# Attention into a capacity-limited expert layer: the gate's VectorE steps moved within and across the slots of a hand-written order

## The chip, the cores and the metric

The kernel runs on one core of one Trainium2 chip. Each core has five engines with queues of their own, worked off in order: TensorE (PE; its weight loads are listed as PEld), VectorE (DVE), ScalarE (ACT), GpSimd (POOL) and SyncE (SP). SP and POOL issue most of the DMA transfers. The metric is the device time of one launch in microseconds; the median of three runs is given, and beside it one execution that was taken with the profiler.

## The reference

Inputs: q, k, v of shape (8, 12, 448, 64) (batch, heads, sequence, head size), gains g_q and g_k of 64, a gate matrix (768, 8), expert weights w1 (8, 768, 1024) and w2 (8, 1024, 768), capacity 80.

```
q_n = q / sqrt(mean(q*q) + 1e-6) * g_q          # the same for k
scores = q_n @ k_n.T / 8
attn = softmax(scores);  a = attn @ v            # (8, 12, 448, 64)
x = a, heads beside each other                   # (3584, 768)
logits = x @ w_gate;  expert = argmax(logits)
gate = max of softmax(logits)
per expert: of its tokens the 80 with the largest gate stay
    out[token] = gate * (relu(x[token] @ w1) @ w2)
all other rows of out are 0
```

## The kernel before, in words

**Groups, rows and slots.** The 96 heads are worked in 24 groups of four heads; three groups make a batch b, so there are 8 batches. A group has 7 rows (64 key positions for each of the two halves u). For a row, `score` (L351) computes transposed scores on PE into a PSUM tile ps, and ACT takes the exponential into an SBUF tile at (L362). `av` (L365) multiplies at with v on PE, added up over the 7 rows into po. `presum` (L387) adds up the at tiles on DVE into sm (L392, L394), whose column sums are the softmax denominators.

A **slot** s is two rows. The loop at L791 writes out, for each slot, in this order: the lists `begins`, the scores of rows 2s and 2s+1, the list `pre`, the presums of rows 2s-2 and 2s-1, the list `mid`, the av of those rows, then the lists `ahead` and `end`. Each engine's queue holds its instructions in the order in which they are written, so the place of a step in these lists is its place on every engine and DMA queue it uses. A list keeps the order in which steps were entered: first the loop over the groups (L717 to L734), then the loop over the batches (L735 to L764). So within one list of a slot a group's steps stand ahead of a gate's. There are 84 slots; group g starts in slot b0 = 7g//2.

**Preparing a group.** q and k are loaded on the SP queue (`load_qk`, L247). ACT squares them (`square`, L266, sq<-qk L270, list `mid` of slots b0-7 for q and b0-6 for k), DVE sums the squares (`squares`, L273, ms<-sq L278, list `end` of the same slots). `rstd` (L286, `mid` of slot b0-5) forms the inverse root: two ACT instructions (Ln L289, Exp L290, both called the root here) and three small DVE ones (L291 to L293). `normalise` (L300, qn, L306 on DVE) follows in the `mid` of b0-5 and b0-4. `transp` (L328, `end` of slot b0-2) turns qn on PE into tp, and ACT copies tp to qkT (L347, L349); for k the tp tile comes from the pool scps, which has two buffers and which the scores, the transposes of k and the merge's scratch tiles share.

**The gate of a batch.** With b0 = (3b+2)*7//2 (so 7, 17, 28, 38, 49, 59, 70, 80): `zl` (L396) forms gate sums and denominators on PE in slot b0+5, `gate1` (L414) copies them (zsb, zo) and adds them on DVE (zsb, L424), `gate1t` (L426, slot b0+6) turns them and ACT copies them to zs. `gate1v` (L439) forms the quotients on DVE: two reciprocals rz (L445) and four products lx (L453); it also issues two SP transfers of rz to DRAM (L460). `gate2` (L465) forms the logits: a reduction lg (L468), the maximum lmax (L471), lex (L474), eq (L476) and a small memset (L477). `gate2x` (L480) is the gate exponential on ACT (L481) and the copy of the kinds eqb (L483). `gate2b` (L486) sums and inverts it on DVE (lsum L489, gw L491). `gate2i` (L494) prepares tiles on POOL; `gate2p` (L515) splits gw on POOL (L518 to L512), waiting for gw.

**The merge.** `merge` (L524) keeps for each expert the 80 best tokens so far. Its steps: `row` (transposes of gw on PE, copied by ACT, L543), `experts` (`kinds`: transposes of eqb), `vbeat` (comparisons on DVE, L550, L553), `vtied` (ties, L559, L561), `own` and `vahead`, `counts` and `vput`, `place`, `turn`. The loop at L755 places them: the first function of a step in `ahead` (or `end` for `row`), the others in `end`.

**Weights.** The weights of experts 0 to 2 are loaded to SBUF by POOL (`fetch_held`, L669, behind a small DVE memset, L671). Those of experts 3 to 7 are first converted to bf16 in DRAM by POOL transfers of half a matrix (`stage_w`, L201, `begins`, 20 of them in slots 36 to 80: for matrix n, counted from 0, slots s = 9 + 23n//5 and s + 2), later fetched on SP.

**After the slots** comes the last batch's merge (L828 on), then the experts, one after the other.

The slot loop, and the functions that the diff touches:

Of the kernel before, what the change touches and what calls it, by code (L numbers as in the profile page):

```python
# [21 lines left out]
def kernel(  # L22
# [210 lines left out]
    with av_stack:  # L233
# [459 lines left out]
        begins, pre, mid, end = {}, {}, {}, {}  # L693

        def at_slot(where, s, f, *a):
            where.setdefault(s, []).append((f, a))
# [3 lines left out]
        def first(s, f, *a):  # L700
            ahead.setdefault(s, []).append((f, a))
# [15 lines left out]
        for g in range(NG):  # L717
            b0 = g * RD // 2
# [16 lines left out]
        for b in range(B):  # L735
            b0 = (NQ * b + NQ - 1) * RD // 2
            if b == B - 1:
                at_slot(end, b0 + 3, zl, b, range(NQ - 1))
                at_slot(end, b0 + 4, xout, NG - 2)
                at_slot(end, b0 + 4, zl, b, range(NQ - 1, NQ))  # L740
                at_slot(end, b0 + 4, gate1, b)
                at_slot(end, b0 + 4, xout, NG - 1)
                at_slot(end, b0 + 5, gate1t, b)
                at_slot(mid, b0 + 6, gate1v, b)
                continue
            first(b0 + 5, zl, b, range(NQ))
            first(b0 + 5, gate1, b)
            at_slot(end, b0 + 6, gate1t, b)
            at_slot(mid, b0 + 7, gate1v, b)
            at_slot(mid, b0 + 7, gate2, b)  # L750
            at_slot(mid, b0 + 8, gate2i, b)
            at_slot(end, b0 + 8, gate2x, b)
            at_slot(pre, b0 + 9, gate2b, b)
            at_slot(pre, b0 + 9, gate2p, b)
            for t, fs in enumerate(merge(b)):  # L755


                if b == B - 2 and t > 3:
                    at_slot(end, b0 + 12 + t, fs[0])
                    continue  # L760
                s = 15 + b % 2 if b < B - 2 else 13
                (first if t else lambda *a: at_slot(end, *a))(
                    b0 + (10, 10, 12, s, 18 + b % 2, 20 + b % 2)[t], fs[0])
                for n, f in enumerate(fs[1:]):  # L764
                    at_slot(end, b0 + (10, 11, 12, s)[t], f)
        at_slot(begins, 0, load_wgs)
        at_slot(end, NS - 6, weights_early)
        at_slot(end, NS, weights_late)
# [8 lines left out]
        for e in range(E):  # L777
            for i in range(2):
                s = 9 + 23 * (2 * e + i) // 5
# [48 lines left out]
    b = B - 1  # L828
# [215 lines left out]
```

## Time and profile before

| | |
|---|---|
| median of 3 runs | 423.92 us (422.47 to 424.89) |
| the profiled execution | 423.0 us |
| its span, first to last instruction | 421.3 us |
| PE busy | 399.1 us (95%) |
| DVE busy | 357.5 us (85%) |
| ACT busy | 314.9 us (75%) |
| POOL busy | 73.5 us (17%) |
| granted TensorE clock | 0.998 of full speed |
| HBM read and written | 335 GB/s over the span |

Busy time is the time with an instruction on an engine; register, semaphore and DMA-issuing instructions don't count. The slots of attention fill about the first 357 us, the last merge and the experts the rest. In the timelines that follow, a line is a run of like instructions: its start, the time to the end of its last, engine, line, operation, tiles, and in brackets the idle time before it with the engine and line that ended it. Instructions overlap a little at their ends, so a start may lie before the end of the one ahead. Times in the rows are microseconds from the start of the span.

### The profile page before, as it was taken

The numbers are of one execution on the slowest core, as the hardware profiler recorded it, in microseconds if no ns is written. First come the engines' busy times: TensorE is split into PE (matmuls) and PEld (weight loads), VectorE is DVE, ScalarE is ACT, GpSimd is POOL, SyncE is SP. The second block draws the span as 40 slices with busy tenths as digits, with TensorE's granted clock in tenths as the row PEclk, the third lists the DMA queues.
The fourth block names the chain that finished last, engine by engine and source line by source line (L and its number), as shares of the span: only waits on it lengthen the run. The fifth ranks groups of instructions, "written<-read, shape, count | busy, mean of one in ns | idle before, by whom it ended". The sixth has DMA issues, their size and how long they took to land.

```text
span 421.3 us, 12543 instructions
## 1 busy us (share of the span) xinstructions
PE 399.1 (95%) x5289; PEld 194.9 (46%) x5289; DVE 357.5 (85%) x641; ACT 314.9 (75%) x479; POOL 73.5 (17%) x118
## 2 busy tenths in 40 slices
PE   6799999999989999999899999999999999889993
PEld 6334444444444445444444444443444443448882
DVE  5699889998999999989999999989999779735550
ACT  5898979997889799979798799878997784202120
POOL 2000001301040205100420024001500050134321
PEclk9999999999999999999999999999999999999999
DMA  7355599999959999999799969999799298869981
GB/s 261 123 149 140 152 224 317 282 254 268 287 166 206 326 230 274 242 237 320 234 236 233 338 172 195 232 286 338 170 237 312 59 358 211 270 213 339 342 301 47
DMA packets 75983, 100.91 MB, mean 240 GB/s; under 512 B 8344, under 2 KB 65176, under 8 KB 75928
## 3 DMA queue, kind: packets, MB, share of 16 engines
q1 hardware_dynamic: 59856, 70.53, 52.2%
q0 software_dynamic: 15776, 29.13, 36.1%
q8 instruction: 41, 0.67, 0.6%
q10 hardware_dynamic: 296, 0.46, 0.4%
q14 instruction: 14, 0.11, 0.1%
HBM read 101.11 MB, written 39.89 MB: 335 GB/s over the span
## 4 chain that ended last, share of the span: by engine, by line
PE 69%; DMA 12%; DVE 10%; ACT 5%; issue 2%; SPq 0%; POOLq 0%; DVEq 0%; ACTq 0%
PE ps L359 26%; PE po L376 26%; DMA w_sb<-wb_scratch 5%; PE zl L411 4%; DMA qk<-in_k_dram 4%; PE tp L314 3%; PE xp L314 3%; DVE ms L278 2%; DVE sm L394 2%; DMA xr_scratch<-xb 2%; PE py L992 1%; DVE qn L306 1%; PE ph L973 1%; ACT qkT L349 1%; DMA xg<-xr_scratch,idxG 1%
## 5 line engine op out<-in xcount | busy, mean ns | idle before, releaser
L359 PE MATMUL ps<-qkT 64*64 64x448 f32 x1344 | 147.9, 548 | 7.6 <-ACT qkT L349 3.2
L362 ACT ACTIVATE at<-ps 128x896 f32<-128x896 f32 x168 | 146.4, 931 | 2.5 <-PE ps L359 1.6
L376 PE MATMUL po<-at,vt 64*64 64x448 f32 x1344 | 142.4, 537 | 0.1
L394 DVE TENSOR_TENSOR sm<-sm,at 128x896 f32<-128x896 f32 x120 | 132.0, 1100 | 2.9
L376 PEld LDWEIGHTS po<-at,vt 64*64 64x64 f32 x1344 | 50.0, 133 | 74.9 <-issue 64.3
L359 PEld LDWEIGHTS ps<-qkT 64*64 64x64 f32 x1344 | 43.1, 132 | 73.2 <-issue 23.5
L278 DVE TENSOR_REDUCE ms<-sq 128x14 f32<-128x896 f32 (+1 forms) x50 | 51.9, 1044 | 6.6 <-ACT sq L270 6.4
L306 DVE TENSOR_TENSOR qn<-qk,rs 128x896 f32<-128x896 f32 (+1 forms) x50 | 52.5, 1052 | 1.9
L270 ACT ACTIVATE sq<-qk 128x896 f32<-128x896 f32 (+1 forms) x50 | 46.3, 929 | 2.8 <-DMA qk<-in_q_dram 2.8
L518 POOL CAST pt<-gw 128x4 bf16<-128x4 f32 x8 | 6.9, 866 | 201.9 <-DVE gw L491 201.9
L977 ACT ACTIVATE h_sb<-ph 128x320 bf16<-128x320 f32 x16 | 7.0, 437 | 39.8 <-PE ph L973 39.8
L654 ACT COPY xb<-xp 128x1024 f32<-128x1024 f32 x24 | 24.3, 1011 | 9.7 <-PE xp L314 9.6
L314 PEld LDWEIGHTS tp<-ident,qn 64*128 64x128 f32 x672 | 23.4, 139 | 11.1 <-issue 5.3
L314 PE MATMUL tp<-ident,qn 64*128 64x64 f32 x672 | 26.9, 226 | 0.0
L383 ACT COPY us<-po 128x896 f32<-128x896 f32 (+1 forms) x24 | 21.4, 893 | 6.2 <-PE po L376 6.2
L392 DVE TENSOR_TENSOR sm<-at 128x896 f32<-128x896 f32 x24 | 25.9, 1081 | 0.0
L347 ACT ACTIVATE qkT<-tp,gqk 128x896 f32<-128x896 f32 x23 | 23.5, 1023 | 0.0
L349 ACT COPY qkT<-tp 128x896 f32<-128x896 f32 x24 | 21.9, 913 | 1.3 <-PE tp L314 1.2
L992 PE MATMUL py<-w_sb,h_sb 128*80 128x384 bf16 (+1 forms) x136 | 22.2, 317 | 0.6 <-DMA w_sb<-wb_scratch 0.6
L996 DVE TENSOR_SCALAR yo<-py,gwT 80x384 f32<-80x384 f32 (+1 forms) x16 | 9.5, 600 | 14.9 <-PE py L992 14.7
L411 PE MATMUL zl<-us,wgs 64*32 64x448 f32 x192 | 21.0, 540 | 0.0
L411 PE MATMUL zl<-sm,zsel 64*32 64x448 f32 x192 | 20.5, 540 | 0.0
(170 smaller groups left out, 412.0 us busy)
## 6 DMA issues: line engine op xcount, KB each, us to landing
wb_scratch<-in_moe_w_dram POOLq DMA_DIRECT2D x20, 768.0 KB, 14.9
w_sb<-wb_scratch SPq DMA_DIRECT2D x9, 1536.0 KB, 8.1
vt<-in_v_dram SPq DMA_DIRECT2D x24, 448.0 KB, 6.3
out_dram<-zeros SPq DMA_DIRECT2D x28, 384.0 KB, 8.2
qk<-in_q_dram SPq DMA_DIRECT2D x23, 448.0 KB, 5.0
qk<-in_k_dram SPq DMA_DIRECT2D x23, 448.0 KB, 6.6
xr_scratch<-xb SPq DMA_DIRECT2D x48, 192.0 KB, 10.2
w_sb<-in_moe_w_dram POOLq DMA_DIRECT2D x6, 1536.0 KB, 15.7
```

Source lines behind the costliest of these rows:

```text
L270: nc.scalar.activation(st[g]["sq%d" % a][:, lo:hi], st[g]["qk"][a][:, lo:hi], AF.Square)
L278: nc.vector.reduce_sum(out=st[g]["ms"][:, a, lo:hi], in_=st[g]["sq%d" % a][:, lo:hi], axis=AX.X)
L306: nc.vector.tensor_mul(qn[:].rearrange("p (x hh) d -> p hh x d", hh=2)[:, h0:h1], qk[:, lo:hi].rearrange("p (hh x) d -> p hh x d", x=NX), ...
L314: nc.tensor.transpose(o, w, one[p, p], tile_position=(p.start, 0))
L349: nc.scalar.copy(T[:], tp[:, :, :S])
L359: nc.tensor.matmul(ps[u * 64:u * 64 + 64, hh, :S], T1[d, u, x * 64:(x + 1) * 64], T0[d, u, :], start=True, stop=True)
L362: nc.scalar.activation(at[:], ps[:, :, :S], AF.Exp)
L376: nc.tensor.matmul(po[u][hh * D:(hh + 1) * D, u, :S], vt[p, hh * NX + x, :], at[p, hh, :], start=(x == 0), stop=(x == RD - 1))
L392: nc.vector.tensor_add(s["sm"][:], s["at0"][:], s["at1"][:])
L394: nc.vector.tensor_add(s["sm"][:], s["sm"][:], s["at%d" % x][:])
L411: nc.tensor.matmul(t[32 * c:32 * c + 32, r, :S], w, x, start=(i == 0), stop=(i == NQ - 1))
L992: nc.tensor.matmul(py[:, :c1 - c0], h_sb[:, fc, :], chunk(e, 1, fc)[:, c0:c1], start=(fc == 0), stop=(fc == FC - 1))
```

## The change

`gate1v` and `gate2` stood in the list `mid` of slot b0+7. `gate1v` goes to the list `end` of the same slot, behind that slot's `squares`; `gate2` and `gate2i` go to the `end` of slot b0+8, behind its `squares`; `gate2x` goes from the end of slot b0+8 to that of b0+9, `gate2b` and `gate2p` from the `pre` of b0+9 to that of b0+10. In the merge, `vtied` is the second of the other functions of step 1: with `11 + n` it goes from the end of slot b0+11 to that of b0+12, while `vbeat` stays. The last batch (b = 7) is placed by lines of its own and is not touched. No instruction is added or removed.

```diff
--- before.py
+++ after.py
@@ -746,12 +746,12 @@
             first(b0 + 5, zl, b, range(NQ))
             first(b0 + 5, gate1, b)
             at_slot(end, b0 + 6, gate1t, b)
-            at_slot(mid, b0 + 7, gate1v, b)
-            at_slot(mid, b0 + 7, gate2, b)
-            at_slot(mid, b0 + 8, gate2i, b)
-            at_slot(end, b0 + 8, gate2x, b)
-            at_slot(pre, b0 + 9, gate2b, b)
-            at_slot(pre, b0 + 9, gate2p, b)
+            at_slot(end, b0 + 7, gate1v, b)
+            at_slot(end, b0 + 8, gate2, b)
+            at_slot(end, b0 + 8, gate2i, b)
+            at_slot(end, b0 + 9, gate2x, b)
+            at_slot(pre, b0 + 10, gate2b, b)
+            at_slot(pre, b0 + 10, gate2p, b)
             for t, fs in enumerate(merge(b)):
 
 
@@ -762,7 +762,7 @@
                 (first if t else lambda *a: at_slot(end, *a))(
                     b0 + (10, 10, 12, s, 18 + b % 2, 20 + b % 2)[t], fs[0])
                 for n, f in enumerate(fs[1:]):
-                    at_slot(end, b0 + (10, 11, 12, s)[t], f)
+                    at_slot(end, b0 + (10, 11 + n, 12, s)[t], f)
         at_slot(begins, 0, load_wgs)
         at_slot(end, NS - 6, weights_early)
         at_slot(end, NS, weights_late)
```

## Rows read from the trace of the kernel before

**Rows 1.** page: shares of the span on the chain, by engine

```profile
PE 69%; DMA 12%; DVE 10%; ACT 5%; issue 2%; SPq 0%; POOLq 0%; DVEq 0%; ACTq 0%
```

**Rows 2.** PE timeline, 96 to 126 us: start, us, instructions, [idle before <-releaser]

```profile
119.24 0.98 PE L359 MATMUL ps<-qkT 64*64 64x448 f32 x8 [1.24 <-ACT qkT L349]
...
122.42 0.43 PE L314 MATMUL mp<-ident,gw 64*128 64x64 f32 x8
```

**Rows 3.** ACT timeline, same stretch (first gate of an odd batch, b = 1)

```profile
114.47 0.23 ACT L481 ACTIVATE lex<-lex 128x32 f32<-128x32 f32 x1 [0.96 <-DVE lex L474]
...
115.04 1.72 ACT L362 ACTIVATE at<-ps 128x896 f32<-128x896 f32 x2
117.81 0.32 ACT L289 ACTIVATE rs<-ms,eps 128x28 f32<-128x28 f32 x1 [1.06 <-DVE ms L278]
```

**Rows 4.** DVE timeline, same stretch

```profile
101.70 0.63 DVE L424 TENSOR_TENSOR zsb<-zsb,zo 128x448 f32<-128x448 f32 x1 [1.54 <-ACT zo L423]
...
112.00 0.46 DVE L445 RECIPROCAL rz<-zs 128x24 f32<-128x24 f32 x2
...
113.14 0.85 DVE L468 TENSOR_REDUCE lg<-lx 128x32 f32<-128x384 f32 x1
...
114.70 1.09 DVE L278 TENSOR_REDUCE ms<-sq 128x14 f32<-128x896 f32 x1
...
116.70 1.08 DVE L278 TENSOR_REDUCE ms<-sq 128x14 f32<-128x896 f32 x1
...
121.86 2.47 DVE L394 TENSOR_TENSOR sm<-sm,at 128x896 f32<-128x896 f32 x2
```

**Rows 5.** PE timeline, 268 to 302 us (b = 5)

```profile
294.11 0.98 PE L359 MATMUL ps<-qkT 64*64 64x448 f32 x8 [0.69 <-ACT qkT L349]
```

**Rows 6.** busy: length, PE, PEld, DVE, ACT, POOL; PEclk, DMA share, GB/s

```profile
162.00:174.00 12.00, 12.00 (x157) 4.87 (x151) 11.76 (x20) 11.90 (x21) 7.96 (x12) 1.00 1.02 255
```

**Rows 7.** DVE timeline, 165 to 190 us (even batch, b = 2)

```profile
172.33 1.08 DVE L278 TENSOR_REDUCE ms<-sq 128x14 f32<-128x896 f32 x1
```

**Rows 8.** ACT timeline, same stretch

```profile
173.50 0.34 ACT L289 ACTIVATE rs<-ms,eps 128x28 f32<-128x28 f32 x1
...
174.02 0.43 ACT L574 COPY own<-mp 128x320 f32<-128x320 f32 x1
```

**Rows 9.** PE timeline, same stretch

```profile
174.80 1.73 PE L359 MATMUL ps<-qkT 64*64 64x448 f32 x16
```

**Rows 10.** DVE timeline, 56 to 99 us (b = 0)

```profile
67.14 0.46 DVE L445 RECIPROCAL rz<-zs 128x24 f32<-128x24 f32 x2
...
72.51 1.09 DVE L278 TENSOR_REDUCE ms<-sq 128x14 f32<-128x896 f32 x1 [0.56 <-ACT sq L270]
74.40 0.19 DVE L489 TENSOR_REDUCE lsum<-lex 128x4 f32<-128x32 f32 x1 [0.81 <-ACT lex L481]
```

**Rows 11.** ACT timeline, same stretch

```profile
68.25 0.97 ACT L270 ACTIVATE sq<-qk 128x896 f32<-128x896 f32 x1
...
86.08 0.34 ACT L289 ACTIVATE rs<-ms,eps 128x28 f32<-128x28 f32 x1
```

**Rows 12.** POOL timeline, 204 to 215 us

```profile
209.64 2.98 POOL L204 DMA_DIRECT2D wb_scratch<-in_moe_w_dram  x4
```

**Rows 13.** DMA issues between 229.8 and 230.3 us: KB each, us to landing

```profile
qk<-in_q_dram SPq DMA_DIRECT2D x1, 448.0 KB, 8.2
```

**Rows 14.** ACT timeline, 240 to 276 us (b = 4)

```profile
242.52 0.97 ACT L270 ACTIVATE sq<-qk 128x896 f32<-128x896 f32 x1
```

**Rows 15.** DMA queues, 257 to 281 us: packets, MB, share of 16 engines

```profile
q0 software_dynamic: 2277, 3.78, 85.5%
q1 hardware_dynamic: 1821, 1.74, 26.5%
```

**Rows 16.** DMA queues, 233 to 241 us

```profile
q1 hardware_dynamic: 2257, 2.97, 104.2%
```

**Rows 17.** DVE timeline, 240 to 276 us

```profile
243.24 0.46 DVE L445 RECIPROCAL rz<-zs 128x24 f32<-128x24 f32 x2
```


## The prediction

> **What bounds the kernel now.** I read the chain of waits first: 69% of the span on it is PE and 10% DVE [rows 1]. So TensorE sets the pace, and the question is where it waits. PE's timeline over the gate of the second batch (b = 1, slots 22 to 28) shows it: the second half of a slot's scores idles 1.24 us for ScalarE's copy qkT [rows 2], which frees the PSUM buffer the scores want. ScalarE's timeline says why the copy was late [rows 3]: the Ln of the root (L289) idled 1.06 us for the sums of squares, and earlier the gate's exponential idled 0.96 us for VectorE's logits, with the slot's exponentials queued behind it. VectorE's timeline of that stretch [rows 4] closes the ring: between the normalise that ends at 112.00 and the squares at 114.70 stand the gate's quotients (1.14 us, up to lg at 113.14) and its logits (1.56 us). The same wait comes back one odd batch later (b = 3) and, with 0.69 us of idle, in b = 5 [rows 5]; even batches show none.
>
> The last thing to see is that VectorE has nearly no room either. In a stretch of an even batch it is busy 11.76 of 12.00 us, beside 12.00 of PE [rows 6], and in b = 1 and b = 2 it stops for another engine only once per two batches, the 1.54 us before zsb [rows 4]. A tidier order moves its work but removes none.
>
> **Part 1, the odd batches.** Behind the change VectorE does, from 112.00: squares (1.00: the 2.00 from 114.70 to 116.70 hold these squares and one add of the same length), quotients 1.14, the add 1.00, second squares at 115.14 instead of 116.70 [rows 4]. They are 1.56 us earlier, the price of the logits. The root on ScalarE starts at 117.81 - 1.56 = 116.25 and the copies follow it. ScalarE is free by then, as the 0.96 us wait for the logits is gone. TensorE can win at most its idle 1.24. But the gate's exponential and the kinds' copy now stand behind those copies, in front of the next exponentials: 0.57 us (114.47 to 115.04 [rows 3]), so ScalarE hands on 1.56 - 0.57 = 0.99. **About 1.0 us each in b = 1 and b = 3.** In b = 5 the idle of 0.69 is the limit; I take **0.65**.
>
> A new wait could take this place: gw. Its reduce and reciprocal now follow the normalise that ends at 121.86 [rows 4], and the transposes of gw into a row, at 122.42 before [rows 2], would come at 121.4. TensorE then waits some 0.5 us in order. Behind it stand the next slot's scores, but their second half needs ScalarE's copy of the row, and ScalarE first copies xb, a transpose issued ahead of gw's. That copy covers it, so I cost it at 0, up to 0.5 per odd batch if the cover is gone.
>
> **Part 2, the even batches take most of it back.** From zsb at 101.70 to the squares at 172.33 VectorE runs the same work in either order, so those squares still end at 173.41 [rows 7]. The root behind them started at 173.50 [rows 8]: a slack of under 0.1. If TensorE and ScalarE arrive 1.0 earlier, the root simply waits. What can be won is the slack from the root to the next scores: these stand at 174.80 [rows 9], and their buffer comes free with the copy of own, 174.02 + 0.43 = 174.45 [rows 8], which comes with the root, no more than 0.1 earlier: 174.4. **Kept: 0.4 of 1.0** (between 0.1, the slack of the root alone, and 1.0). In b = 6 no later root needs VectorE, so b = 5's 0.65 reaches the end; the expert weights there are issued as the experts finish and move along.
>
> Ties one slot later put the second squares of the odd phase ahead of them: no cost; without that the root there would wait 1.06 us of VectorE longer. The counts that read the ties come at least one slot after. The last gate (b = 7) is not touched. For b = 6 there are no squares left, so its moved steps keep their order.
>
> **Part 3, the first batch loses.** In b = 0 VectorE is not late but early: it began the quotients at 67.14 [rows 10], while ScalarE's square of that slot ran from 68.25 for 0.97 [rows 11]. The gate's 2.7 us had covered that. Now VectorE waits 69.22 - 67.14 = 2.1 for it. The old idles of 0.56 (second squares) and 0.81 (exponential) [rows 10] go. Net 0.7 late, up to the root at 86.08 [rows 11], which has no slack. Of that the 0.35 between the copy of own and the scores is absorbed as in rows 8 and 9: **+0.35** (0 to 0.7).
>
> **Part 4, POOL and the transfers.** gate2p is moved past one slot's start, so POOL's wait for gw moves past a staging transfer whenever one is issued there: slots 38, 59 and 80. POOL runs far ahead of the slots and is held only by gw, so staging comes in bursts behind it. Counted from the code, the bursts behind b = 2, 3, 4, 5, 6 change from 5, 4, 5, 4, 1 transfers to 4, 5, 4, 5, 0, and each starts about 3.9 us later (gw's place before, behind the squares of 116.70 plus 1.0 and two small steps, 118.0, against 121.9). The one that can hurt is behind b = 3, four transfers at 209.64 [rows 12]: its fifth meets the load of q for b = 4, which took 8.2 us [rows 13] from its issue at 229.85 to 238.05, against the square of b = 4 at 242.52 [rows 14]. In a burst the staging queue moved 3.78 MB in 24 us, so a transfer of 0.79 MB takes 5.0 us; SP's queue beside it got 1.74 MB [rows 15], 0.073 MB per us, and alone 2.97 MB in 8 us [rows 16], 0.371. The fifth transfer thus costs SP's queue 5.0 x (1 - 0.073/0.371) = 4.0 us: q lands at 242.1. The other end is the whole shift, 3.9 + 5.0: 246.9. I take 242.6, near the first, because SP's bytes get through before the later start. The square then ends at 243.6 and VectorE, which wants it at 243.24 [rows 17], loses 0.35: **b = 3's gain shrinks from 0.4 to 0.1.** The rz stores on SP go out 1.0 us later; the loads queued behind them are wanted slots later: 0, at most that 1.0 where a load has no margin.
>
> **Sum.** +0.35 - 0.4 - 0.1 - 0.65 = -0.8 us. The profiled execution took 423.0 (span 421.3 and 1.7 around it), so 422.2; it stands 0.9 under the median of the runs, 423.92, which gives 423.1.
>
> **Rivals.**
> 1. *TensorE keeps everything.* If the roots of the even batches find slack, the odd gains stay: -1.0 - 1.0 - 0.65, and +0.35 or 0 for b = 0: 421.3 to 421.6. For it: PE holds 69% of the chain, DVE 10%. Against: rows 6 to 9. Chance 0.21.
> 2. *VectorE alone is the bound.* No cycle of two batches shortens; only b = 5 wins: -0.65 + 0.35, so 423.6. For it: the 11.76 of 12.00. Against: the 1.54 of idle per cycle and the chain, which runs through PE for the 12 us before the next odd gate. Chance 0.15. The Trainium skill ("Perfetto Trace Analysis", Identifying the Most-Contended Engine) says to judge VectorE by occupancy and to work on the engine with most of it, while matmul busy time tells little for TensorE; by that rule a reorder that takes no work off VectorE wins nothing in the cycles, this rival's 423.6. The trace agrees with it for that stretch.
> 3. *Slower: q of b = 4 comes late.* At 246.9 its square ends at 247.9, VectorE waits 4.6, of which 0.4 is absorbed; +4.2 + 0.35 - 0.4 - 0.65 = +3.5: 427.4. It is slower by over 0.5% once q lands after 245.5. For it: the squares stand in front of the gate's work there, with nothing left to cover them. Against: the byte count of part 4. Chance 0.13.
>
> **Numbers.** Forecast 0.51 (its own range 422.4 to 424.2: kept gains 0.1 to 0.65, q between 242.1 and 244). About 0.5%, 2.1 us, is what a measurement of this kernel can tell from no change. Faster by that is rival 1, and a little of the forecast: 0.22. Slower is rival 3's part beyond 245.5 and mishaps in b = 0: 0.14. The rest, 0.64. The range from 421.2 to 425.8 takes in rival 1, the forecast, rival 2 and rival 3 up to a landing near 245.
>
> **What would show it.** Right: the wait of rows 2 shrinks to near 0 in b = 1 and 3, ScalarE's wait for logits is gone, and instead the root (L289) waits for squares of the even batches some 0.5 to 1.0 us and VectorE's idle of 1.54 before zsb shrinks by no more than 0.5; VectorE idles 2 us for the square of b = 0; the burst near 213 has five transfers. Wrong: no new wait at the even roots and a period of two batches 1.0 shorter (rival 1); an idle of VectorE of 2 us or more for the square of b = 4 (rival 3); a PE wait for gw that the next scores inherit.

## The result, and the profile after the change

The change made the kernel slower: 427.18 us (median of 12 runs, 424.6 to 430.11) against 423.86 for the kernel before (12 runs beside it, 422.23 to 424.89), ratio 1.0086, interval 1.0061 to 1.0111. The forecast of 423.1 and its whole range were missed, on the side that it gave 0.14. The profiled execution took 424.98 with a span of 423.2, against 421.3 before; 1.9 us can so be followed in the trace, of the 3.3 between the medians. Executions of one kernel differ (before by 2.7 us, after by 5.5) with the mean granted clock of the run (after: 424.6 to 425.0 at 0.993, 426.9 to 430.1 at 0.976 to 0.985), so terms of less than a microsecond are read from the trace.

The best ruler in it is the copy of the gate sums (ScalarE's first zsb<-zl, L421), once per batch. Its starts, as differences from batch to batch, show where the time went:

| us | b0-1 | b1-2 | b2-3 | b3-4 | b4-5 | b5-6 | rest of the span |
|---|---|---|---|---|---|---|---|
| before | 40.44 | 46.39 | 41.03 | 46.41 | 41.03 | 46.41 | 99.33 |
| after | 40.50 | 45.31 | 41.31 | 45.93 | **45.96** | 45.30 | 98.50 |

The gate of an odd batch stands at the start of the stretches b1-2, b3-4 and b5-6, and there the change works: 1.1 us less where nothing else disturbs (in b3-4 another load of q held ScalarE for 1.11 us). Each even stretch gives 0.28 back. One stretch, the gate of b = 4, costs 4.9 and more than eats the rest. (The last column moves between 98.5 and 100.2 from run to run, in kernels that are alike there, so its 0.8 is not counted for the change. Where it is 100 or more, the granted clock is 0.91 to 0.97 in a 20 us window between 360 and 400 us.)

**The chain.** The page of the changed kernel gives, as shares of the span on the chain by engine:

```profile
PE 61%; DVE 24%; DMA 7%; issue 3%; ACT 3%; POOLq 0%; DVEq 0%; ACTq 0%
```

Beside [rows 1], PE has lost 8 points and VectorE gained 14. DMA's share was larger before, but by line most of it is now qk<-in_q_dram, 6% of the span, which before was not among the lines that the page names. Here is that load, from the DMA issues between 225.2 and 225.6 us (KB each, us from issue to landing), and what SyncE and GpSimd put into the queues around it (SP timeline, 200 to 247 us, and POOL timeline):

```profile
qk<-in_q_dram SPq DMA_DIRECT2D x1, 448.0 KB, 19.7
```

```profile
214.70 2.90 SPq L774 DMA_DIRECT2D out_dram<-zeros  x2
...
225.26 0.77 SPq L242 DMA_DIRECT2D qk<-in_q_dram  x1
228.01 0.37 SPq L242 DMA_DIRECT2D qk<-in_k_dram  x1
228.43 5.31 SPq L774 DMA_DIRECT2D out_dram<-zeros  x1
```

```profile
212.56 2.97 POOL L204 DMA_DIRECT2D wb_scratch<-in_moe_w_dram  x4
...
216.00 0.81 POOL L204 DMA_DIRECT2D wb_scratch<-in_moe_w_dram  x1
```

Five staging transfers in one burst, as the prediction counted, and later than the four of [rows 12]. The q of group 18, whose square stands beside the gate of b = 4 (the prediction's "q for b = 4"), is issued at 225.26 and lands at 244.96, after 19.7 us where it took 8.2 [rows 13]. Counted from the gate sums of b = 3 (187.51, before 188.12) it is issued 4.0 us earlier than before and lands 7.5 later. What waits for it, in the ScalarE, VectorE and PE timelines of the same stretch:

```profile
244.98 0.95 ACT L270 ACTIVATE sq<-qk 128x896 f32<-128x896 f32 x1 [3.41 <-DMA qk<-in_q_dram]
```

```profile
245.96 1.09 DVE L278 TENSOR_REDUCE ms<-sq 128x14 f32<-128x896 f32 x1 [3.42 <-ACT sq L270]
```

```profile
240.31 1.68 PE L376 MATMUL po<-at,vt 64*64 64x448 f32 x16
...
246.78 3.13 PE L376 MATMUL po<-at,vt 64*64 64x448 f32 x16 [3.28 <-ACT us L383]
```

The square [rows 14] stops ScalarE's queue for 3.41 us; the copy of us stands behind it, and that copy frees the PSUM buffer that TensorE's next output sums want. So TensorE idles 3.28, and then sixteen matmuls take 3.13 us where sixteen of the same kind took 1.68 just before. The windows say why (length, busy PE, PEld, DVE, ACT, POOL; PEclk, DMA share, GB/s):

```profile
241.00:245.00 4.00, 2.50 (x28) 0.76 (x20) 1.44 (x2) 0.59 (x2) 0.00 (x0) 1.00 1.08 345
245.00:249.00 4.00, 2.22 (x12) 0.79 (x16) 3.04 (x8) 4.00 (x5) 0.00 (x0) 0.66 1.06 395
249.00:253.00 4.00, 4.00 (x68) 2.18 (x64) 3.64 (x9) 2.28 (x5) 0.00 (x0) 0.92 1.02 313
```

The granted clock falls to 0.66 behind the idle stretch: a part of it ran at 1.2 in place of 2.4 GHz. Idle 3.28 and matmuls 3.13 - 1.68 = 1.45 make 4.7 of the 4.9 us.

**The odd gates** look as intended. VectorE and ScalarE around the gate of b = 1 (96 to 126 us), to be read against [rows 3, 4]:

```profile
112.22 1.08 DVE L278 TENSOR_REDUCE ms<-sq 128x14 f32<-128x896 f32 x1
...
115.22 1.08 DVE L278 TENSOR_REDUCE ms<-sq 128x14 f32<-128x896 f32 x1
```

```profile
116.34 0.32 ACT L289 ACTIVATE rs<-ms,eps 128x28 f32<-128x28 f32 x1 [0.61 <-DVE ms L278]
...
118.57 0.23 ACT L481 ACTIVATE lex<-lex 128x32 f32<-128x32 f32 x1
```

The second squares start 1.48 us earlier, the root too, the exponential waits for nothing. On PE the idle 1.24 [rows 2] is gone, and the wait for gw (the gate weights) that the prediction named is there:

```profile
122.18 0.45 PE L314 MATMUL mp<-ident,gw 64*128 64x64 f32 x8 [0.54 <-DVE gw L491]
```

### The profile page after: what moved, and what is told of

The parts are those of the page before. It is cut to its first block, busy times and chain, and to the rows that moved or that the text cites. A ratio compares the mean times of both kernels' runs of the same rounds, so it can differ in the third digit from the quotient of the medians.

```text
span 423.2 us, 12547 instructions
## 1 busy us (share of the span) xinstructions
PE 400.6 (95%) x5289; PEld 195.7 (46%) x5289; DVE 356.4 (84%) x641; ACT 314.8 (74%) x479; POOL 71.0 (17%) x118
## 4 chain that ended last, share of the span: by engine, by line
PE 61%; DVE 24%; DMA 7%; issue 3%; ACT 3%; POOLq 0%; DVEq 0%; ACTq 0%
PE ps L359 21%; PE po L376 21%; DVE sm L394 8%; DMA qk<-in_q_dram 6%; PE py L992 4%; PE zl L411 4%; DVE qn L306 4%; DVE ms L278 3%; PE ph L973 3%; PE tp L314 3%; PE xp L314 2%; DVE sm L392 1%; DMA vt<-in_v_dram 1%; DMA xg<-xr_scratch,idxG 1%; DVE beat L550 1%
## 5 line engine op out<-in xcount | busy, mean ns | idle before, releaser
L376 PE MATMUL po<-at,vt 64*64 64x448 f32 x1344 | 143.9, 542 | 3.5 <-ACT us L383 3.5
L394 DVE TENSOR_TENSOR sm<-sm,at 128x896 f32<-128x896 f32 x120 | 130.3, 1086 | 2.9
```

What stands on the lines that cost most here:

```text
L376: nc.tensor.matmul(po[u][hh * D:(hh + 1) * D, u, :S], vt[p, hh * NX + x, :], at[p, hh, :], start=(x == 0), stop=(x == RD - 1))
L394: nc.vector.tensor_add(s["sm"][:], s["sm"][:], s["at%d" % x][:])
```

## The experiments

The first four separate the burst from VectorE's order. The start of the burst and the landing of q are counted in us from the gate sums of b = 3, since the kernels are not equally far along by then:

| | bursts behind b = 2 to 6 | burst behind b = 3 starts | q of group 18 landed | b4-5 |
|---|---|---|---|---|
| before | 5, 4, 5, 4, 1 | 21.5 | 49.9 | 41.03 |
| burst alone | 4, 5, 4, 5, 0 | 21.5 | 53.9 | 41.03 |
| four each | 4, 4, 4, 4, 2 | 25.1 | 54.1 | 41.79 |
| after | 4, 5, 4, 5, 0 | 25.1 | 57.5 | 45.96 |
| late alone | 4, 5, 4, 5, 0 | 25.2 | 57.7 | 45.51 |
| stores moved | 4, 5, 4, 5, 0 | 25.1 | 52.3 | 41.35 |

**1. Four to each burst.** The changed kernel, with four staging transfers issued elsewhere:

```diff
-                    at_slot(begins, s + 2 * half, stage_w, e, i, half)
+                    t = s + 2 * half
+                    late = {59: 59, 68: 69, 78: 80, 80: 80}
+                    if t in late:
+                        at_slot(pre, late[t], stage_w, e, i, half)
+                    else:
+                        at_slot(begins, t, stage_w, e, i, half)
```

> The changed kernel, with four staging transfers (slots 59, 68, 78, 80) issued at another place on GpSimd's queue, so that the bursts behind the gates of b = 2 to 6 hold 4, 4, 4, 4, 2 transfers in place of 4, 5, 4, 5, 0. Theory A (the fifth transfer of the later burst holds the load of q for group 18, and TensorE then runs at a lower granted clock for some us): q of group 18 lands at 241 or before, ScalarE's 3.4 us wait for it goes, the granted clock stays near 1.0 in 245 to 253, and the time is 420.7 to 421.9, 5 to 6 below the changed kernel's 427.2 and 2 to 3 below the kernel before. Rival B (VectorE's new order itself costs the time, the late q only fills the idle that it makes): 426 to 428. Rival C (the burst costs its time, but VectorE is the bound elsewhere and the new order brings nothing): 423.5 to 424.3.

Measured: 420.4 us, ratio 0.9939 (0.9915 to 0.9962). VectorE's order is innocent of the 4.9 us: with the same order, b4-5 is 41.79 and this kernel is faster than both. Two details of the expectation were off: the time is 0.3 below its range, and q lands only at 242.8, not at 241, so that ScalarE and PE still lose a little (their timelines):

```profile
242.82 0.95 ACT L270 ACTIVATE sq<-qk 128x896 f32<-128x896 f32 x1 [0.65 <-DMA qk<-in_q_dram]
```

```profile
244.61 1.74 PE L376 MATMUL po<-at,vt 64*64 64x448 f32 x16 [0.53 <-ACT us L383]
```

After an idle of 0.53 the matmuls keep their 1.7 us.

**2. The fifth transfer alone**, at the old start times and with the old order on VectorE (kernel before):

```diff
-                    at_slot(begins, s + 2 * half, stage_w, e, i, half)
+                    t = s + 2 * half
+                    at_slot(begins, t - (t in (38, 59, 80)), stage_w, e, i, half)
```

> The kernel before, with three staging transfers (slots 38, 59, 80) issued one slot earlier, so that its bursts hold 4, 5, 4, 5, 0 transfers as in the changed kernel, but start where they did and with the old order on VectorE. Theory A in the form that the fifth transfer alone is enough: q of group 18 lands after 244 and the time is 426 to 428. Theory A in the form that it takes the later start too: q lands between 240 and 242.5, before its square is due, and the time is 423.4 to 424.9, no change. Rival B (the order of VectorE): no change as well.

Measured: 423.77 us, ratio 0.9996 (0.9971 to 1.0021): no change. q took 12.4 us, landed at 242.5, and its square began at 242.95 without a wait:

```profile
qk<-in_q_dram SPq DMA_DIRECT2D x1, 448.0 KB, 12.4
```

The fifth transfer costs q 4.0 us, and the margin is just wide enough for it.

**3. The delayed part alone.** The kernel before, with `gate2i` at the end of slot b0+8, `gate2x` at the end of b0+9, `gate2b` and `gate2p` in the `pre` of b0+10 and the ties at `11 + n`; quotients and logits stay in `mid`:

```diff
-            at_slot(mid, b0 + 8, gate2i, b)
-            at_slot(end, b0 + 8, gate2x, b)
-            at_slot(pre, b0 + 9, gate2b, b)
-            at_slot(pre, b0 + 9, gate2p, b)
+            at_slot(end, b0 + 8, gate2i, b)
+            at_slot(end, b0 + 9, gate2x, b)
+            at_slot(pre, b0 + 10, gate2b, b)
+            at_slot(pre, b0 + 10, gate2p, b)
...
-                    at_slot(end, b0 + (10, 11, 12, s)[t], f)
+                    at_slot(end, b0 + (10, 11 + n, 12, s)[t], f)
```

> The kernel before, with only the delayed part of the change: the gate's exponential, kinds, ties and the wait for gw one slot later; its quotients and logits stay where they were. The bursts then hold 4, 5, 4, 5, 0 and start about 3 us later than before. Theory A: q of group 18 lands between 243.5 and 245.5, the same wait on ScalarE and VectorE appears there, and with no gain in the odd batches the time is 427 to 430. Rival B (VectorE's order): 423.3 to 424.9, as before.

Measured: 428.38 us, ratio 1.0103 (1.0061 to 1.0146). The loss at b = 4 is here whole, without VectorE's new order: q lands at 246.7 (later than the 245.5 expected at most, as this kernel has gained nothing on the way and even lost some 0.4 us in each odd stretch), and PE and the windows show the same two pieces:

```profile
248.52 3.20 PE L376 MATMUL po<-at,vt 64*64 64x448 f32 x16 [2.61 <-ACT us L383]
```

```profile
245.00:249.00 4.00, 1.39 (x16) 0.39 (x12) 3.35 (x12) 2.27 (x3) 0.00 (x0) 0.96 1.06 387
249.00:253.00 4.00, 4.00 (x48) 1.86 (x42) 2.82 (x3) 2.12 (x4) 0.00 (x0) 0.62 1.08 362
```

**4. VectorE's order alone.** The changed kernel with exponential, row and wait for gw in their old slots:

```diff
-            at_slot(end, b0 + 9, gate2x, b)
-            at_slot(pre, b0 + 10, gate2b, b)
-            at_slot(pre, b0 + 10, gate2p, b)
+            at_slot(end, b0 + 8, gate2x, b)
+            at_slot(pre, b0 + 9, gate2b, b)
+            at_slot(pre, b0 + 9, gate2p, b)
```

> The changed kernel with the gate's exponential, the row of gw and the wait for gw back in their old slots, so that only the order on VectorE is new (quotients and logits behind the squares) and the bursts hold 5, 4, 5, 4, 1 as before, starting some 1 to 3 us later than before. Theory A: the long wait for q of group 18 is gone (it lands before 242.5); ScalarE's exponential now waits some 2 us for the logits with the slot's exponentials behind it, so the odd gains go and the time is 423 to 425. Rival B (VectorE's order itself costs the 4 us at b = 4): 427 or more, with the loss at b = 4 as in the changed kernel.

Measured: 432.41 us, ratio 1.0179 (1.0131 to 1.0226). The time is far above theory A's and in rival B's range, but the loss is not at b = 4 as B has it: q of group 18 is not late (b4-5 is 41.13), so VectorE's order is again not what costs b = 4. Instead b1-2 grows from 46.39 to 49.17, b3-4 from 46.41 to 48.06 and b5-6 from 46.41 to 49.41. ScalarE's timeline and the list of waits say why:

```profile
119.32 0.23 ACT L481 ACTIVATE lex<-lex 128x32 f32<-128x32 f32 x1 [3.80 <-DVE lex L474]
```

```profile
ACT lex L481 <- DVE lex L474: 12.4, 5, 3.8
```

TensorE, behind it, stops for 2.79 us, and the granted clock falls there as well (PE timeline and a window):

```profile
120.85 1.75 PE L314 MATMUL tp<-ident,qn 64*128 64x64 f32 x28 [2.79 <-ACT at L362]
```

```profile
122.00:124.00 2.00, 2.00 (x20) 0.96 (x20) 1.83 (x5) 1.77 (x3) 1.01 (x4) 0.50 0.12 44
```

The wait for the logits was put at 2 us and the loss at no more than the odd gains; it is up to 3.8, in ScalarE's queue, and the odd stretches are 1.7 to 3.0 us longer than before. The two halves of the change need each other: the order on VectorE only pays with the later exponential, and that one brings the later wait for gw.

**5. SyncE's bytes.** The changed kernel, bursts untouched, with two stores of zeros out of q's way:

```diff
-            at_slot(begins, 9 + 5 * i // 2, lambda i=i: nc.sync.dma_start(
+            at_slot(begins, {16: 57, 17: 58}.get(i, 9 + 5 * i // 2), lambda i=i: nc.sync.dma_start(
```

> The changed kernel, with two of SyncE's stores of zeros (384 KB each, due in slots 49 and 51, issued at 214.7 us) moved to slots 57 and 58; the bursts of staging transfers stay as in the changed kernel, five of them behind b = 3. Theory A (the load of q for group 18 stands in SyncE's queue behind these bytes, which move at some 0.07 MB per us beside the burst: 0.77 MB are 10 us): q lands before 241, ScalarE's and VectorE's waits of 3.4 us go and the granted clock stays near 1.0 in 245 to 253; the time is 420.3 to 422.3. Rival B (q gets through only when the burst is over, whatever stands before it): q lands after 243.5 and the time is 425 to 428.

Measured: 420.16 us, ratio 0.9937 (0.9911 to 0.9962), just below theory A's range and the lowest median of the versions that leave nothing out, though four each at 420.4 can't be told from it. q takes 14.9 us, its square starts at 240.77 and waits for nothing, and the granted clock is 1.00 in all three windows from 241 to 253:

```profile
qk<-in_q_dram SPq DMA_DIRECT2D x1, 448.0 KB, 14.9
```

So 0.79 MB less ahead of it brought q 57.5 - 52.3 = 5.2 us forward, not 10. The rate assumed was about right: beside the burst SyncE's queue moved 2.22 MB in 27 us in the changed kernel (215.5 to 242.5), 0.08 MB per us. But here that queue fell empty inside the burst: the next stores of xb are issued at 221.41, and from 221 to 225 us it moved next to nothing (DMA queues):

```profile
q1 hardware_dynamic: 13, 0.01, 0.9%
```

So some 4 of the 10 us went unused. No stretch loses to a load of q any more: 40.52, 45.31, 41.33, 45.31, 41.35, 45.30.

**6. One transfer moved**, that of slot 59 alone (`late = {59: 59}` in the edit of experiment 1):

> The changed kernel, with only the staging transfer of slot 59 issued behind the wait of b = 4 instead of ahead of it: the bursts behind b = 2 to 6 hold 4, 4, 5, 5, 0 transfers. Theory A (only the burst behind b = 3 meets a load without margin): time from the gate sums of b = 4 to those of b = 5 41.3 to 42.0 us, as with four in each burst, the others unchanged, 420.2 to 421.3. Rival B (every later start of five transfers costs, as a load of q behind each is just as tight): another stretch of 41 or 45 us is longer by 2 us or more, 423 to 427.

Measured: 420.47 us, ratio 0.9951 (0.993 to 0.9972); b4-5 is 41.51, all others as in experiment 5. The two bursts of five that still start late, behind b = 4 and 5, cost nothing: one transfer more in one late burst, ahead of one load with little margin, made the change slow. This time can't be told from that of experiment 5 either.

**7 and 8. Odd batches only.** The gates of even batches go back to their old places, first with the staging as it was, then with that of experiment 1:

```diff
+            o = b % 2
-            at_slot(end, b0 + 7, gate1v, b)
+            at_slot(end if o else mid, b0 + 7, gate1v, b)
...
-            at_slot(pre, b0 + 10, gate2p, b)
+            at_slot(pre, b0 + 9 + o, gate2p, b)
...
-                    at_slot(end, b0 + (10, 11 + n, 12, s)[t], f)
+                    at_slot(end, b0 + (10, 11 + n * o, 12, s)[t], f)
```

> The change made for the odd batches only (b = 1, 3, 5); b = 0, 2, 4, 6 keep the old places. The staging transfers are not touched; their bursts hold 5, 4, 5, 4, 1 as in the kernel before, and only those of four start later. From the gate sums of one batch to those of the next the kernel before takes 41.03 us behind an even batch and 46.4 behind an odd one; the changed kernel 41.31 and 45.31. Theory A (the 0.28 us that the changed kernel loses behind an even batch come from the gate's new place there): 41.0 and 45.3, and 0.5 for q of group 18 at most; 419.6 to 420.8. Rival B (VectorE has the same work in either order and bounds the even batches, as the prediction has it): 41.3 to 41.7 behind the even batches; 420.8 to 422.4.

> The change for the odd batches only, as in the run beside it, and the four staging transfers (slots 59, 68, 78, 80) in the places that they have in the run with four to each burst. Theory A: as the run beside it, with the wait for q of group 18 unchanged, as the burst ahead of it holds four either way; 419.4 to 420.6. Rival B (VectorE bounds the even batches): 420.4 to 421.5.

Measured: 421.3 (0.9963, 0.9939 to 0.9987) and 421.45 (0.9946, 0.9922 to 0.9971). The times miss theory A and lie in rival B's ranges. So do the stretches: b2-3 is 41.31 and 41.30, the same as with the even gates moved. The 0.28 does not come from the gate's place there. From the gate sums of b = 1 to those of b = 3 it is 86.6 us with either placing, against 87.4 before: something bounds the pair of batches. (In run 7, other loads of q were late, up to 1.28 us at 283.61, and b5-6 lost 0.8; which load is late varies from run to run.)

**9 to 11. Is VectorE that bound?** One normalise done twice in each of two pairs of batches, on top of experiment 5 and of the kernel before; then one add left out:

```diff
-            for lo, hi in parts:
+            for lo, hi in parts * (2 if g in (10, 16) and a else 1):
                 h0, h1 = lo // NX, hi // NX
```

```diff
-            elif x > 1:
+            elif x > 1 and not (g in (9, 15) and x == 4):
                 nc.vector.tensor_add(s["sm"][:], s["sm"][:], s["at%d" % x][:])
```

> The run with the two stores moved (420.2), with one normalise (L306, 1.09 us on VectorE, some 1.0 from start to start) done twice in groups 10 and 16, once in each of the two pairs of batches from the gate sums of b = 1 to those of b = 3 and from b = 3 to b = 5, far from any gate. A pair takes 86.6 us there, 87.4 in the kernel before. Theory A (VectorE bounds the pair of the new order, as the prediction's part 2 has it): each pair 0.8 to 1.0 us longer, the time 421.7 to 422.3. Rival B (TensorE bounds it): a pair longer by 0.2 at most, 420.0 to 420.7.

> The kernel before with the same normalise done twice in groups 10 and 16. Theory A in the prediction's form (VectorE had under 0.1 us of slack at the root of the even batches in the old order too): each pair 0.6 to 1.0 us longer than its 87.4, the time 1.2 to 2.0 above before. Rival B (in the old order the wait of the odd gates bounds the pair and VectorE has room): 0 to 0.5 a pair, the time at most 0.8 above before.

> The run with the two stores moved, with one add of VectorE left out (L394, 1.08 us) in groups 9 and 15, once in each pair of batches; this leaves one term out of two sums of the softmax. Theory A (VectorE bounds the pair): each pair shorter by 0.2 to 0.6, as far as TensorE's small wait behind the even root (0.16 us) and ScalarE's (0.4 us) reach: 86.0 to 86.4, the time 418.9 to 419.8. Rival B (TensorE bounds it): 86.6 a pair, 420.0 to 420.4.

| us | pair b = 1 to 3 | pair b = 3 to 5 | median |
|---|---|---|---|
| before | 87.42 | 87.44 | 422.84 |
| before, one normalise more | 88.07 | 87.78 | 423.47 |
| stores moved (new order) | 86.64 | 86.66 | 420.16 |
| new order, one normalise more | 87.74 | 87.74 | 422.13 |
| new order, one add less | 86.35 | 87.43 | 419.67 |

In the new order the extra microsecond is paid whole in the first pair, which is 1.1 longer. The second pair is 1.1 longer too, but is no evidence: in it ScalarE also waited 1.41 us for another load of q (198.41), and the root of b = 4 only 0.63 for VectorE. ScalarE's root and TensorE's scores in b = 2 of experiment 9, and then the same two in the changed kernel, in the place of [rows 8, 9]:

```profile
174.55 0.32 ACT L289 ACTIVATE rs<-ms,eps 128x28 f32<-128x28 f32 x1 [1.01 <-DVE ms L278]
```

```profile
175.49 1.79 PE L359 MATMUL ps<-qkT 64*64 64x448 f32 x16 [0.60 <-ACT own L574]
```

```profile
173.20 0.32 ACT L289 ACTIVATE rs<-ms,eps 128x28 f32<-128x28 f32 x1 [0.44 <-DVE ms L278]
```

```profile
174.14 1.79 PE L359 MATMUL ps<-qkT 64*64 64x448 f32 x16 [0.16 <-ACT own L574]
```

In the old order only 0.65 and 0.34 of it were paid (ratio 1.0021, 0.9994 to 1.0048), so a pair had some 0.35 to 0.65 us of room there. The first pair fits theory A, the second pair and the time fit rival B. With one add of 1.08 us less, the first pair wins 0.29, within what was expected, so the next limit is close. The second pair is again no evidence: in it ScalarE waited 1.57 us for another load of q (196.54). So VectorE bounds the pair of the new order, shown from both sides, but for the first pair alone.

## Why the prediction was wrong

**The step that failed is in part 4:** "I take 242.6, near the first, because SP's bytes get through before the later start." The bounds were right, 242.1 for the fifth transfer alone and 246.9 with the whole shift of 3.9. The fifth transfer, estimated at 4.0 us, cost 4.0 at the old start (53.9 against 49.9) and 3.4 at the late one. But the later start was put at 0.5 and cost 3.5: between *burst alone* and *after* the burst begins 3.5 later and q lands 3.5 later; with four transfers it lands 4.2 later (54.1 against 49.9). The changed kernel, 0.6 us further along by then, saw q land at 244.96.

The reason given, that SyncE's bytes get through before the later start, was true of a part of them. These are the DMA queues in the 4 us from 24 after the gate sums of b = 3, in burst alone (212.56 to 216.56) and in the changed kernel (211.6 to 215.5):

```profile
q0 software_dynamic: 537, 0.80, 113.8%
q1 hardware_dynamic: 22, 0.02, 1.2%
```

```profile
q1 hardware_dynamic: 443, 0.62, 53.0%
q0 software_dynamic: 15, 0.02, 6.9%
```

SyncE's queue (q1) moved 0.62 MB there instead of 0.02. But GpSimd's staging queue (q0) did not move the 0.80 MB there that it moved in burst alone with the DMA engines nearly to itself. It had to move them later, beside SyncE's queue, and all but 0.04 MB of the five transfers were through at 242.5 in place of 237.0, which is 6.5 us later from the gate sums. From the same 24 us on, SyncE's queue moved 3.7 MB until q landed in either kernel: 0.02, then 1.68 beside the burst and 2.03 behind it in burst alone; 0.62, 2.22 and 0.91 in the changed kernel. The 1.1 MB fewer that were left behind the burst are worth 3.0 us at 0.37 MB per us; 6.5 - 3.0 = 3.5. The prediction counted the bytes that get ahead of a later burst, and left out that the burst itself would end later by more than its shift. That the result equals the shift is chance: with four transfers the same shift cost 4.2.

**Two further terms of rival 3 were too small.** It let the square's lateness reach the end through VectorE (245.96 - 243.24 = 2.7 by its rule, 0.4 absorbed) and named 245.5 as the landing from which it decides. In the changed kernel the square was due earlier, at 244.98 - 3.41 = 241.57 and not at 242.52, because ScalarE had come forward; and what held TensorE was the copy of us behind the square in ScalarE's queue. Then the clock added 1.45 us, which no step had. So q at 244.96, below the 245.5, already cost 4.9 us in its stretch. The late q of rival 3 is what happened, though its cost came through TensorE's stop and the clock and not through VectorE; its chance of 0.13 and the share of slower, 0.14, were too low. That its 427.4 stands beside the 427.18 measured is luck: q landed 2 us earlier than it has it, and 1.4 us of the difference between the medians have no place in the trace.

**Part 1** (odd batches, 1.0 each in b = 1 and 3, 0.65 in b = 5): 1.08, and 1.1 in the other two where no load is late. For b = 5 the limit was read from the one idle row [rows 5]; but its stretch b5-6 was as long before as b1-2 (46.41 and 46.39), so the same was to be won. The wait for gw came, at 0.54 as estimated, and stayed hidden.

**Part 2** (even batches, bound by VectorE, 0.4 kept of 1.0): the bound was right and the size was off, as 0.8 is kept of 1.08. Counted from the gate sums of b = 1, the scores of b = 2 come 0.85 earlier. Of this 0.36 is the slack between the root's copies and the scores, which the prediction put at 0.35, and 0.06 that at the root. The other 0.43 is VectorE's: the prediction let the same work take the same time, but from zsb to the squares of b = 2 it takes 172.09 - 101.89 = 70.20 us where it took 172.33 - 101.70 = 70.63 [rows 4, 7]. VectorE's rows showed no wait in between; a part of the difference lies inside merged rows (two adds in 2.47 us [rows 4], now in 2.19). That these are small waits for ScalarE's tiles was not shown. The extra normalise in the kernel before moves those squares by its whole 1.00 in the first pair (173.28 - 101.65 = 71.63), and only the 0.35 behind the root is left to absorb it. The rule that rival 2 took from the Trainium skill ("Perfetto Trace Analysis", Identifying the Most-Contended Engine) holds for the new order, by the first pair of experiments 9 and 11. It did not for the old one, where a reorder that takes no work off VectorE still won 0.8 us a pair.

**Part 3** (b = 0, +0.35): VectorE waits 2.03 us for the square, predicted 2.1, but b0-1 is only 0.06 longer. The root comes at 86.58, 0.5 after [rows 11] and 0.4 of it after the start of the kernel is set off (gate sums of b = 0 at 60.39 and 60.26), not 0.7; the 0.35 that the next scores absorb is nearly all of that.

**The sum**, in the terms of the text: +0.06 for +0.35; -0.8 for -0.4; b = 3 with its q +4.45 for -0.1; -1.11 for -0.65; with the start (+0.13) and the last stretch (-0.83) +1.9, the difference of the spans. The rest between this and the medians, 1.4 us, lies between runs: 424.98 was the second shortest of the twelve. Where the longer ones lose it stays open, as only one has a trace.

## What to carry to other kernels

When a step that releases a burst of transfers is moved, look at what the shared queues carry before, during and behind the new burst, up to the landing that matters. Bytes that get ahead of a later burst are only one side; a burst that is no longer alone at its start also ends later. Price a late load by everything queued behind its first reader on that reader's engine, and by the slower matmuls that may follow TensorE's stop. And when a reorder pays on one engine but a neighbouring transfer takes the gain, moving the transfer is worth more than taking the reorder back: two stores moved turned +0.9% into -0.6%.

## What was not expected of the hardware

In all the traces TensorE stopped for 2 us or more five times between 60 and 345 us, and its granted clock fell behind four of these stops: 3.28 us (after) and 2.61 us (late alone), each followed by sixteen matmuls in 3.13 and 3.20 us instead of 1.68; 2.79 us (order alone), with 28 transposes in 1.75 instead of 1.08; and 2.04 us (order alone, b = 5), with a clock of 0.67 and 0.50 in the windows from 301 to 305. Behind the fifth, as long as the third, it stayed at 1.00 in every window from 209 to 220 (order alone, b = 3, PE timeline):

```profile
211.15 1.08 PE L314 MATMUL tp<-ident,qn 64*128 64x64 f32 x28 [2.80 <-ACT at L362]
```

That stretch, b3-4, is 1.1 us shorter than b1-2 of the same run. Stops of 0.53 us (four each) and of 1.24 us [rows 2] were followed by no fall. In the changed kernel's trace the late load so cost almost half as much again as its wait; whether every execution pays this is not shown.

Beside a staging burst, where both DMA queues had work, they got nearly equal numbers of packets, not of bytes. So it is in the changed kernel (DMA queues, 229 to 241 us: packets, MB, share of 16 engines), where GpSimd's packets are larger, and in burst alone, with 1809 and 1773 from 216.56 to 237:

```profile
q0 software_dynamic: 1009, 1.80, 79.9%
q1 hardware_dynamic: 1012, 1.07, 31.5%
```

The Trainium skill ("DMA: Bandwidth & Descriptors", Queues, rings and completion order) states that an engine takes turns between queues packet by packet; the trace agrees in that the packets counted by the profile are nearly equal in number. With 1.06 KB a packet against 1.78, SyncE's queue gets the smaller share of the bytes beside a staging burst.
